# Retention with routed experts on one core: the steps in pairs, four places for rows on their way out, one for the sums

## The chip, the cores and the metric

The kernel runs on one core of one Trainium2 chip. TensorE (PE) multiplies matrices, VectorE (DVE), ScalarE (ACT) and GpSimd (POOL) work on tiles in SBUF and PSUM, and the queue of SyncE (SP) starts most transfers; ACT and POOL start some of their own. The metric is the device time of one execution in microseconds (us). Before the change the median of three runs is 399.14 us (398.21 to 399.93). A second execution, the profiled one, took 400.5 us.

## The reference

Eight heads of retention on 8 sequences of 576 tokens, then a layer of eight experts, each token going to one of them or to none:

```python
scores = scale * np.matmul(q, k.transpose(0, 1, 3, 2))
Dmat = np.where(rel >= 0, gamma[:, None, None] ** rel[None], 0.0)   # decay by distance, causal
x = np.matmul(scores * Dmat[None], v)                               # 4608 tokens x 512
do_compute = x @ w_skip > 0
e_idx = np.argmax(x @ w_gate, axis=1)                               # one expert of 8
y[mask] = gate_w * (np.maximum(xc[mask] @ w1[e], 0.0) @ w2[e])
out = x + y                                                         # y only where do_compute
```

## The kernel before, in words

The program has two parts. The first makes x, 36 tiles of 128 tokens (g = 0 to 35, nine tiles for each pair of sequences), writes it to `out` and finds each token's expert. The second runs the experts, with weights and values split into a high and a low part, three products for one. The change is in the first part alone.

**A tile.** Two transfers on SP's queue bring tile g into one of five places of `u` (`load_half`, L511): first queries and keys, then values and keys by rows. A place comes free when the tile that was five earlier is done with. PE multiplies queries by keys (`by_quarters`, L569, into `psc` and `ps_q`), and DVE and ACT put the decayed scores in place (`decay`, into `u` and `sq`). POOL scales the keys (`keys`, `kn`, L612) and the values (`rows_of`, `vs`, L634); ACT adds to `vs` the running state that PE has summed in `ps_s` (`state`, L648, copied at L663). PE then makes the tile's result in `pxt` from two groups of products, `second` (L680) and `values` (L704). `scale` (L718) is DVE's product of `pxt` with a table `gt_sb`; it puts the result into `xt`, which holds four tiles and has two places. `stage_c` (L724) turns a tile on PE (`px`), ACT copies it to `xn` (L726, two places) and asks on its own queue for the store to `out` (L727).

**A step** is one round of the loop over n and deals with two tiles; it begins with n = -1, a round without results to finish. After every second step `logits_to` multiplies the four tiles in `xt` by the gate's weights (`pl`, copied by ACT to `lt`), and in the next step `logits_from` turns the result (`pn`), reduces it on DVE (`lg`, L748) and calls `route`, whose `route_a` (L186 to L207) finds maxima and marks on DVE. `table(n)` and `growth(n)` (L544) make the tables `dq_sb` and `gt_sb` for tiles to come.

**What sets the order.** PE runs in the order in which the code is written (`tc.manual_schedule`). On the other engines a scheduler orders the operations by their needs, starting from the order of the code, and adds the waits on semaphores. Every transfer also takes one of eight lanes in turn, and waits until the lane's transfer before it has landed. PE's products are 32 bits wide, so each one in the code is two in the trace, with a load of weights each.

After the last tile PE goes to the experts: `turn_early`, `up_early`, and then up and down products in one stream (L463). That part stands as it was.

Of the kernel before, what the change touches and what calls it, by code (L numbers as in the profile page):

```python
# [12 lines left out]
F32 = mybir.dt.float32  # L13
# [10 lines left out]
NTOK, DM, NE, DF = B * S, H * D, 8, 1024  # L24
P = 128
NT = NTOK // P
HALF = S // P * 2
NQ = HALF + 1
NPR = H // 2
# [57 lines left out]
def kernel(  # L87
# [25 lines left out]
    def keep_up(n):  # L113
        for _ in range(n):
            nc.tensor.matmul(ps_m, warm[:, :P], warm, start=True, stop=True)
# [375 lines left out]
    with ExitStack() as actx:  # L491
# [35 lines left out]
        def last_product():  # L527
            return next(i for i in reversed(nc.cur_bb.bb.instructions) if i.engine == mybir.EngineType.PE)
# [18 lines left out]
        def table(n):  # L547
            times(dq_sb[:, n], mt_sb.unsqueeze(1).broadcast_to([P, NPR, D]), TQ + n, D)

        def growth(n):  # L550
            if n < NCH - 1:
                times(gt_sb[:, n], gt_sb[:, 0], TG + n, P)
            else:
                for c in range(2):
                    times(gt_sb[:, n, :, c * D : (c + 1) * D], gt_sb[:, 0, :, c * D : (c + 1) * D], TG + n + c, D)
# [23 lines left out]
        def by_quarters(g, own):  # L579
            scores(g)  # L580
            far = [score(g, 1)]
            others = itertools.chain.from_iterable(own + far if g % 2 else far + own)
            for _ in score(g, 0):
                for _ in itertools.islice(others, 1 + len(own)):
                    pass
            for _ in others:
                pass

        def decay(g):

            q = first(g)
            near, far = psc_t.pop(g)
            sc_t[g] = ap.tile([P, NPR, D], F32, tag="sq", name=f"sq_{g}", bufs=3)
            if g % 2 == 0:
                nc.vector.tensor_tensor(sc_t[g], far, dq_sb[:, g % NQ // 2], ALU.mult)
            for j in range(2):
                h = halves[1 - j]
                nc.vector.tensor_tensor(  # L598
                    u_t[g][h, j, :, :D], near[h, :, :D], mt_sb[h].unsqueeze(1).broadcast_to([D, NPR, D]), ALU.mult
                )  # L600
                if q.stop > D:
                    nc.scalar.copy(u_t[g][h, j, :, D:], near[h, :, D:])  # L602
            if g % 2:
                nc.vector.tensor_tensor(sc_t[g], far, dq_sb[:, g % NQ // 2], ALU.mult)

        def keys(g):
            i = g % NQ
            if i == HALF:
                return
            kn_t[g] = ap.tile([P, NPR, P], F32, tag="kn", name=f"kn_{g}")  # L610
            k = TK + i // 2 * 2
            nc.gpsimd.tensor_tensor(  # L612
                kn_t[g].rearrange("p a (j i) -> p a j i", j=2),
                u_t[g][:, 3].rearrange("p a (j i) -> p a j i", j=2),
                tt_sb[:, k : k + 2, :].rearrange("p j a -> p a j").unsqueeze(3).broadcast_to([P, NPR, 2, D]),
                ALU.mult,
            )
# [7 lines left out]
            for j in range(2):  # L625
                nc.gpsimd.memset(vs_t[g][halves[j], j], 0.0)

        def rows_of(g):

            if 1 < g and g % NQ < 2:  # L630
                clear(g)
            for j in range(2):
                h = halves[1 - j]
                nc.gpsimd.tensor_tensor(  # L634
                    vs_t[g][h, j],
                    u_t[g][h, 2, :, j * D : (j + 1) * D],
                    tt_sb[h, TV + g % NQ // 2, :].unsqueeze(2).broadcast_to([D, NPR, D]),
                    ALU.mult,
                )
# [50 lines left out]
        def in_turn(*products):  # L690

            products = list(products)
            while products:
                products = [p for p in products if next(p, p) is not p]
# [3 lines left out]
        def values(g):  # L698

            pxt, opens = sums(g)  # L700
            q = first(g)
            for a in range(NPR):
                for j in range(2):
                    nc.tensor.matmul(  # L704
                        pxt[halves[j], a, q],
                        vs_t[g][:, j, a, :],
                        u_t[g][:, j, a, q],
                        start=opens and a == 0,
                        stop=not opens and a == NPR - 1,
                        skip_group_check=True,  # L710
                    )
                yield

        def scale(g):
            b, o = divmod(g, NB)
            if o == 0:
                xt_t[b] = ap.tile([P, NPR, NB * P], F32, tag="xt", name=f"xt_{b}")
            nc.vector.tensor_tensor(xt_t[b][:, :, o * P : (o + 1) * P], px_t[g], gt_sb[:, g % NQ // 2], ALU.mult)  # L718

        def stage_c(g, tag="xn"):  # L720
            b, o = divmod(g, NB)
            px = pp.tile([P, DM], F32, tag=tag, name=f"px_{g}")
            for c in range(NCC):
                nc.tensor.transpose(px[:, c * P : (c + 1) * P], xt_t[b][:, c, o * P : (o + 1) * P], ident)  # L724
            xn = ap.tile([P, DM], F32, tag="xn", name=f"xn_{g}")
            nc.scalar.copy(xn.rearrange("t (p c) -> t p c", c=NCC), px.rearrange("t (c p) -> t p c", c=NCC))  # L726
            nc.scalar.dma_start(out[g * P : (g + 1) * P, :], xn)  # L727

# [15 lines left out]
        def logits_b(b, lt):  # L744
            pn = pp.tile([P, NB, P], F32, tag="xn", name=f"pn_{b}")
            for o in range(NB):
                nc.tensor.transpose(pn[:, o, :], lt[:, o * P : (o + 1) * P], ident)
            nc.vector.tensor_reduce(  # L748
                lg[:, b * NB : (b + 1) * NB, :],
                pn.rearrange("p t (c w) -> p t w c", w=WP)[:, :, :NW, :],  # L750
                axis=AX.X,
                op=ALU.add,
            )
# [100 lines left out]
        def logits_to(b, tag):  # L854
            nonlocal lt
            lt = b, logits_a(b, tag)

        def logits_from():
            nonlocal lt
            if lt is not None:  # L860
                logits_b(*lt)
                route(lt[0])
                lt = None

        def loaded(g, s, after=None):
            if 3 < g < NT:
                load_half(g, s, after)

        def have(products, g, *args):
            return [products(g)] if 0 <= g < NT else []  # L870

        def ahead(g, do):
            if 0 <= g < NT:
                do(g)
# [4 lines left out]

        for n in range(-1, NT // 2 - 1):
            e = 2 * n
            g = e + 2
            for i in range(2):
                by_quarters(e + 2 + i, have(second, e + i))
                if n < 0:
                    keep_up(NKEEP[i])
                decay(e + 2 + i)
                if n < 0:  # L890
                    keys(i)
                if i == 0:
                    loaded(e + 5, 0)
                    if n > 0:
                        scale(e)
                    if n >= 0:
                        rows_of(e + 3)
                else:
                    loaded(e + 5, 2, last_product())
            if n < 0:  # L900
                rows_of(0)
                rows_of(1)
            if 0 <= n + 2 < NCH:
                table(n + 2)
            if 0 <= n < NCH - 1:
                growth(n + 1)
            if n % 2 == 0:
                routing(1)
                logits_from()
            weights()  # L910
            in_turn(state(e + 2))
            in_turn(*([values(0)] if n == 0 else []), *have(values, e + 1))
            if n == 0:
                scale(0)
            if n >= 0:
                scale(e + 1)
            loaded(e + 6, 0)
            ahead(e + 4, keys)
            if n >= 0:
                ahead(e + 4, rows_of)  # L920
            in_turn(*have(values, e + 2 if n >= 0 else -1))
            in_turn(state(e + 3))
            loaded(e + 6, 2, last_product())
            ahead(e + 5, keys)
            if n < 0:
                rows_of(2)
            else:
                stage_c(e, "xo")
                stage_c(e + 1)
                routing(6 if g < starts[KCUT + 1] else 8)  # L930
                if n % 2:
                    logits_to(n // 2, f"sc{n % 2}")
            weights()
        g = NT
        for i in (2, 1):
# [13 lines left out]
        up_early(0)  # L949
        routing(8)  # L950
        logits_from()
        up_early(1)
        up_early(2)
        routing(8)
# [502 lines left out]
```

## Time and profile before

| what | us |
|---|---|
| median of three runs | 399.14 (398.21 to 399.93) |
| the profiled execution | 400.5 |
| its span (first to last instruction) | 398.8 |
| PE busy in the span | 363.8 |
| DVE, ACT, POOL busy | 276.4, 181.7, 151.2 |
| bytes moved | 106.15 MB |

All times of the rows below are from the span's start; 1.7 us of the execution lie outside the span. A row of a timeline gives an instruction's start, its duration, its engine and line, output and input, and in brackets how long the engine had been idle before it and what ended that. "issue" in such a place says that no semaphore was found that ended it.

### The profile page before, as it was taken

The page shows a single profiled execution, that of the slowest core. Times are in us where ns is not written, and L with a number is a line of the kernel's source. Part 1 is how long each engine was busy: PE and PEld are TensorE (multiplying, and loading weights), DVE is VectorE, ACT ScalarE, POOL GpSimd, SP SyncE. Part 2 cuts the span into 40 slices and gives each one's busy share as a digit, 9 for nine tenths or more (in the row PEclk, how much of TensorE's full clock was granted, in tenths as well). Part 3 has the DMA queues.
Part 4 walks back from the last instruction along what each step waited for, and adds up shares of the span by engine and source line. Part 5 has one row for each costly group of instructions (what it writes and reads, how often), then busy time and mean ns, then how long its engine had stood idle before and what let it go on. Part 6 is the DMA issues. An engine that isn't in the chain of part 4 may idle for free.

```text
span 398.8 us, 12381 instructions
## 1 busy us (share of the span) xinstructions
PE 363.8 (91%) x4884; PEld 335.4 (84%) x4885; DVE 276.4 (69%) x615; ACT 181.7 (46%) x369; POOL 151.2 (38%) x211
## 2 busy tenths in 40 slices
PE   7579889888989887899999999999999999999992
PEld 3477777766868776779899999999999999999992
DVE  3555677566756977696965867866867868677763
ACT  2345354454445453603743543545455545554411
POOL 5856656454754638724044200330320421101032
PEclk9999999999999999999999999999999999999997
DMA  8699999799899896607788886979789998886511
GB/s 309 260 330 315 353 324 323 245 338 341 284 339 334 308 355 217 217 29 234 226 292 256 299 236 220 319 224 353 231 257 355 307 293 284 264 279 212 159 66 59
DMA packets 49572, 106.15 MB, mean 266 GB/s; under 512 B 6102, under 2 KB 21206, under 8 KB 49511
## 3 DMA queue, kind: packets, MB, share of 16 engines
q1 hardware_dynamic: 40951, 85.81, 64.1%
q0 software_dynamic: 3232, 9.99, 7.5%
q10 hardware_dynamic: 5328, 9.52, 6.4%
q8 instruction: 40, 0.66, 0.7%
q14 instruction: 21, 0.17, 0.1%
HBM read 83.51 MB, written 22.28 MB: 265 GB/s over the span
## 4 chain that ended last, share of the span: by engine, by line
PE 57%; DMA 19%; issue 13%; DVE 5%; POOL 2%; ACT 2%; SPq 1%; ACTq 0%; POOLq 0%; DVEq 0%
PE py L463 17%; PE ph L463 16%; DMA out<-rs,sidx 8%; PE pxt L704 5%; DMA out<-xn 5%; PE ps_s L648 3%; PE psc L569 3%; DMA u<-qkv 3%; PE px L724 3%; PE pxt L680 2%; DMA xg<-out,gidx 2%; PE ps_q L569 2%; DMA xh<-hop 1%; PE pl L732 1%; PE ph_early L463 1%
## 5 line engine op out<-in xcount | busy, mean ns | idle before, releaser
L169 DVE TENSOR_TENSOR wlo_w<-w,whi_w 128x1024 fp32r<-128x1024 f32 x59 | 72.0, 1224 | 38.2 <-ACT whi_w L168 37.0
L168 ACT CAST whi_w<-w 128x1024 fp32r<-128x1024 f32 x59 | 61.7, 1049 | 32.8 <-PE py L463 31.5
L463 PE MATMUL py<-hlo,whi_w 128*128 128x336 f32 (+6 forms) x224 | 67.8, 303 | 0.0
L463 PE MATMUL ph<-xhi,wlo_w 128*128 128x336 f32 (+6 forms) x224 | 67.6, 302 | 0.0
L463 PE MATMUL ph<-xlo,whi_w 128*128 128x336 f32 (+6 forms) x224 | 67.5, 302 | 0.0
L463 PE MATMUL ph<-xhi,whi_w 128*128 128x336 f32 (+6 forms) x224 | 67.5, 301 | 0.0
L463 PE MATMUL py<-hhi,wlo_w 128*128 128x336 f32 (+6 forms) x224 | 67.5, 301 | 0.0
L463 PE MATMUL py<-hhi,whi_w 128*128 128x336 f32 (+6 forms) x224 | 67.4, 301 | 0.0
L634 POOL TENSOR_TENSOR vs<-u,tab_sb 64x256 f32<-64x256 f32 x72 | 45.0, 625 | 29.9 <-DMA u<-qkv 17.4
L1079 POOL DMA_INDIRECT out<-rs,sidx x17 | 20.8, 1223 | 83.8 <-DVE rs L1078 82.6
L612 POOL TENSOR_TENSOR kn<-u,tab_sb 128x512 f32<-128x512 f32 x32 | 34.3, 1070 | 32.4 <-DMA u<-qkv 26.2
L471 ACT ACTIVATE hhi<-ph 128x336 fp32r<-128x336 f32 (+8 forms) x61 | 25.9, 424 | 45.3 <-PE ph L463 45.0
L602 ACT COPY u<-psc 64x256 f32<-64x256 f32 x64 | 23.5, 367 | 46.4 <-DVE u L598 37.8
L569 PE MATMUL psc<-u 64*64 64x128 f32 (+1 forms) x576 | 39.1, 273 | 4.7 <-ACT lt L741 3.5
L569 PEld LDWEIGHTS psc<-u 64*64 64x64 f32 x576 | 30.0, 132 | 14.9 <-ACT xn L726 5.9
L463 PEld LDWEIGHTS ph<-xhi,whi_w 128*128 128x128 f32 x224 | 42.3, 189 | 0.1
L463 PEld LDWEIGHTS py<-hlo,whi_w 128*128 128x128 f32 x224 | 42.2, 188 | 0.2 <-DVE hlo L472 0.2
L463 PEld LDWEIGHTS ph<-xlo,whi_w 128*128 128x128 f32 x224 | 42.3, 189 | 0.1
L463 PEld LDWEIGHTS py<-hhi,whi_w 128*128 128x128 f32 x224 | 42.3, 189 | 0.0
L463 PEld LDWEIGHTS ph<-xhi,wlo_w 128*128 128x128 f32 x224 | 42.3, 189 | 0.0
L463 PEld LDWEIGHTS py<-hhi,wlo_w 128*128 128x128 f32 x224 | 42.3, 189 | 0.0
L704 PE MATMUL pxt<-u,vs 128*64 128x128 f32 (+1 forms) x576 | 34.8, 268 | 4.8 <-issue 4.1
(214 smaller groups left out, 710.8 us busy)
## 6 DMA issues: line engine op xcount, KB each, us to landing
u<-qkv SPq DMA_DIRECT2D x68, 512.0 KB
w<-w SPq DMA_DIRECT2D x64, 512.0 KB
out<-xn ACTq DMA_DIRECT2D x36, 256.0 KB
hop<-xg SPq DMA_DIRECT2D x12, 256.0 KB
xh<-hop SPq DMA_DIRECT2D x48, 64.0 KB
hopy<-yp SPq DMA_DIRECT2D x24, 128.0 KB
yr<-hopy SPq DMA_DIRECT2D x6, 512.0 KB
u<-qkv SPq DMA_DIRECT2D x4, 256.0 KB
```

The source lines that it names most:

```text
L168: nc.scalar.copy(hi, t)
L169: nc.vector.tensor_tensor(lo, t, hi.bitcast(F32), ALU.subtract)
L463: nc.tensor.matmul(ps, x, y, start=first and n == 0, stop=last and n == 3 * len(terms) - 1)
L471: nc.scalar.activation(hi, ph, AF.Relu)
L569: nc.tensor.matmul(to[halves[1 - j ^ c], a, : q.stop - q.start], u[halves[j], 1 - j, a, c * D : (c + 1) * D], u[halves[j], j, a, q], start ...
L602: nc.scalar.copy(u_t[g][h, j, :, D:], near[h, :, D:])
L612: nc.gpsimd.tensor_tensor(kn_t[g].rearrange("p a (j i) -> p a j i", j=2), u_t[g][:, 3].rearrange("p a (j i) -> p a j i", j=2), tt_sb[:, k ...
L634: nc.gpsimd.tensor_tensor(vs_t[g][h, j], u_t[g][h, 2, :, j * D : (j + 1) * D], tt_sb[h, TV + g % NQ // 2, :].unsqueeze(2).broadcast_to([D, ...
L648: nc.tensor.matmul(ps_s[halves[j], i % 2, a, :], kn_t[g][:, a, j * D : (j + 1) * D], u_t[g][:, 2, a, j * D : (j + 1) * D], start=i == 0 an ...
L704: nc.tensor.matmul(pxt[halves[j], a, q], vs_t[g][:, j, a, :], u_t[g][:, j, a, q], start=opens and a == 0, stop=not opens and a == NPR - 1, ...
L724: nc.tensor.transpose(px[:, c * P : (c + 1) * P], xt_t[b][:, c, o * P : (o + 1) * P], ident)
L1079: done = nc.gpsimd.indirect_dma_start(out=out, out_offset=bass.IndirectOffsetOnAxis(ap=idx, axis=0), in_=rs[:n], in_offset=None, bounds_ch ...
```

## The change

The loop over n now begins at 0, and what the round n = -1 did is written out ahead of it and in the round n = 0:

- The first three tiles' `vs` (tiles 0, 1 and 2, six operations of 64x256) are made by DVE, not by POOL.
- PE makes the state products of tile 0, the scores of tile 2, the state products of tile 1, and then `values(0)` ahead of the scores of tile 3. Before, both state products stood ahead of the scores, and `values(0)` and `values(1)` came alternating behind the scores of tile 3 and the state products of tile 2.
- The second half of tile 4's load waits for the state products of tile 1, as it did; the load of tile 5 is now written behind `values(0)` and its second half behind the scores of tile 3.
- `scale(e + 1)`, a step's second result, stands ahead of `table` and `growth`, and the call of `route` is a function of its own (`gates`), called behind it.
- `xn` has four places in place of two, and `xt` one in place of two.

```diff
-        def rows_of(g):
+        def rows_of(g, by=nc.gpsimd):
...
-                nc.gpsimd.tensor_tensor(
+                by.tensor_tensor(
                     vs_t[g][h, j],
...
-                xt_t[b] = ap.tile([P, NPR, NB * P], F32, tag="xt", name=f"xt_{b}")
+                xt_t[b] = ap.tile([P, NPR, NB * P], F32, tag="xt", name=f"xt_{b}", bufs=1)
...
-            xn = ap.tile([P, DM], F32, tag="xn", name=f"xn_{g}")
+            xn = ap.tile([P, DM], F32, tag="xn", name=f"xn_{g}", bufs=4)
...
         def logits_from():
+            if lt is not None:
+                logits_b(*lt)
+
+        def gates():
             nonlocal lt
             if lt is not None:
-                logits_b(*lt)
                 route(lt[0])
                 lt = None
...
-        for n in range(-1, NT // 2 - 1):
+        for g in range(2):
+            by_quarters(g, [])
+            keep_up(NKEEP[g])
+            decay(g)
+            keys(g)
+        for g in range(2):
+            rows_of(g, nc.vector)
+        table(1)
+        in_turn(state(0))
+        load_half(4, 0)
+        keys(2)
+
+        for n in range(NT // 2 - 1):
             e = 2 * n
             g = e + 2
...
+            by_quarters(e + 2, have(second, e))
+            decay(e + 2)
+            if n:
+                loaded(e + 5, 0)
+                scale(e)
+                rows_of(e + 3)
+            else:
+                in_turn(state(1))
+                load_half(4, 2, last_product())
+                keys(3)
+                in_turn(values(0))
+                load_half(5, 0)
+                scale(0)
+                rows_of(2, nc.vector)
+            by_quarters(e + 3, have(second, e + 1))
+            decay(e + 3)
+            loaded(e + 5, 2, last_product())
             if n % 2 == 0:
                 routing(1)
                 logits_from()
             weights()
-            in_turn(state(e + 2))
-            in_turn(*([values(0)] if n == 0 else []), *have(values, e + 1))
-            if n == 0:
-                scale(0)
-            if n >= 0:
-                scale(e + 1)
+            if n:
+                in_turn(state(e + 2))
+            in_turn(values(e + 1))
+            scale(e + 1)
+            if n % 2 == 0:
+                gates()
+            if not n:
+                in_turn(state(2))
+                rows_of(3)
+            if n + 2 < NCH:
+                table(n + 2)
+            if n < NCH - 1:
+                growth(n + 1)
             loaded(e + 6, 0)
             ahead(e + 4, keys)
-            if n >= 0:
-                ahead(e + 4, rows_of)
-            in_turn(*have(values, e + 2 if n >= 0 else -1))
+            ahead(e + 4, rows_of)
+            in_turn(values(e + 2))
             in_turn(state(e + 3))
             loaded(e + 6, 2, last_product())
             ahead(e + 5, keys)
-            if n < 0:
-                rows_of(2)
-            else:
-                stage_c(e, "xo")
-                stage_c(e + 1)
...
+            stage_c(e, "xo")
+            stage_c(e + 1)
```

On PE, from the scores of tile 3 to the first transposes, the program had these rows (`ps_s` are state products, `psc` and `ps_q` scores, `pxt_278` and `pxt_302` the results of tiles 0 and 1, `px` the turned tiles; the numbers are the program's names, x8 counts products):

```order
L569 MATMUL psc_299<-u_158 64x128 x2
L569 MATMUL ps_q<-u_158 64x64 x4
L648 MATMUL ps_s<-u_155,kn_245 64x64 x8
L704 MATMUL pxt_278<-u_149,vs_168 64x128 x2
L704 MATMUL pxt_302<-u_151,vs_171 64x128 x2
...
L704 MATMUL pxt_370<-u_155,vs_240 64x128 x8
L648 MATMUL ps_s<-u_158,kn_259 64x64 x8
L724 MATMUL px_393<-ident,xt_361 128x128 x4
```

Now PE has there, from the state products of tile 1 on (`pxt_262` and `pxt_310` are the results of tiles 0 and 1):

```order
L648 MATMUL ps_s<-u_151,kn_225 64x64 x8
L704 MATMUL pxt_262<-u_149,vs_168 64x128 x8
L569 MATMUL psc_307<-u_158 64x128 x2
...
L569 MATMUL ps_q<-u_158 64x64 x4
L704 MATMUL pxt_310<-u_151,vs_171 64x128 x8
L648 MATMUL ps_s<-u_155,kn_245 64x64 x8
L704 MATMUL pxt_370<-u_155,vs_240 64x128 x8
L648 MATMUL ps_s<-u_158,kn_291 64x64 x8
L724 MATMUL px_393<-ident,xt_303 128x128 x4
```

`values(0)` is in front of tile 3's scores, and from `px` on the rows are the same as before. On DVE, in the step with n = 1, the program had (`dq_sb` and `gt_sb` are tables, `xt` the results):

```order
L604 TENSOR_TENSOR sq_471<-ps_q,dq_sb 128x256
L544 TENSOR_TENSOR dq_sb<-tab_sb 128x256
L598 TENSOR_TENSOR u_295<-psc_445,tab_sb 64x4x64
L544 TENSOR_TENSOR gt_sb<-gt_sb,tab_sb 128x512
L718 TENSOR_TENSOR xt_361<-pxt_448,gt_sb 128x4x128
L595 TENSOR_TENSOR sq_577<-ps_q,dq_sb 128x256
```

And now:

```order
L604 TENSOR_TENSOR sq_471<-ps_q,dq_sb 128x256
L598 TENSOR_TENSOR u_301<-psc_445,tab_sb 64x4x64
L718 TENSOR_TENSOR xt_303<-pxt_448,gt_sb 128x4x128
L544 TENSOR_TENSOR dq_sb<-tab_sb 128x256
L544 TENSOR_TENSOR gt_sb<-gt_sb,tab_sb 128x512
L595 TENSOR_TENSOR sq_577<-ps_q,dq_sb 128x256
```

The two table operations have moved behind the result of the step; this is so in the first four steps, after which the tables are complete.

## Rows read from the trace of the kernel before

**Rows 1.** The page: busy time of engines, the instruction queue, shares of the chain
```profile
PE 363.8 (91%) x4884; PEld 335.4 (84%) x4885; DVE 276.4 (69%) x615; ACT 181.7 (46%) x369; POOL 151.2 (38%) x211
...
q8 instruction: 40, 0.66, 0.7%
...
PE 57%; DMA 19%; issue 13%; DVE 5%; POOL 2%; ACT 2%; SPq 1%; ACTq 0%; POOLq 0%; DVEq 0%
```

**Rows 2.** Windows of PE alone: us, busy (instructions), granted clock, DMA share, GB/s
```profile
0.00:163.60 163.60, 136.24 (x3269) 1.00 0.88 309
...
180.00:395.00 215.00, 211.57 (x1492) 1.00 0.77 251
```

**Rows 3.** Chain that ended last, in order of time: start, us, what
```profile
56.44 7.03 DMA out<-xn
...
73.38 8.11 DMA out<-xn
```

**Rows 4.** Timeline of ACT: copies to `xn` that came late
```profile
63.55 0.59 ACT L726 COPY xn<-px 128x512 f32<-128x512 f32 x1 [0.92 <-DMA out<-xn]
...
81.57 0.59 ACT L726 COPY xn<-px 128x512 f32<-128x512 f32 x1 [2.13 <-PE pxt L680]
```

**Rows 5.** Timeline of PE: its waits in the first 27 us
```profile
17.53 1.96 PE L704 MATMUL pxt<-u,vs 128*64 128x128 f32 x31 [1.81 <-issue]
20.16 1.07 PE L704 MATMUL pxt<-u,vs 128*64 128x128 f32 x15 [0.66 <-ACT vs L663]
...
26.10 0.27 PE L680 MATMUL pxt<-sq,u 64*64 64x64 f32 x2 [2.03 <-issue]
```

**Rows 6.** Windows, all engines: us, busy (instructions) of PE, PEld, DVE, ACT, POOL
```profile
17.53:26.09 8.56, 5.87 (x127) 5.25 (x126) 3.60 (x7) 2.99 (x8) 5.25 (x7) 1.00 0.64 217
26.09:41.36 15.27, 14.58 (x378) 12.61 (x379) 9.11 (x20) 7.80 (x19) 9.43 (x15) 1.00 0.96 336
41.37:48.39 7.02, 5.75 (x128) 4.41 (x126) 3.99 (x10) 3.03 (x7) 4.19 (x6) 1.00 0.96 340
48.40:54.19 5.79, 4.90 (x125) 4.53 (x126) 5.08 (x12) 2.39 (x7) 4.09 (x6) 1.00 0.99 348
```

**Rows 7.** Windows, all engines, as rows 6: the transfers around 18 us
```profile
14.00:16.00 2.00, 0.79 (x17) 0.66 (x18) 1.94 (x5) 0.73 (x2) 1.85 (x3) 1.00 1.02 401
16.00:18.00 2.00, 0.47 (x9) 0.46 (x10) 1.89 (x2) 0.37 (x1) 1.92 (x3) 1.00 0.19 70
18.00:20.00 2.00, 1.50 (x27) 1.25 (x22) 0.68 (x2) 0.62 (x2) 1.93 (x3) 1.00 0.00 0
...
22.00:39.00 17.00, 14.29 (x353) 12.30 (x352) 9.98 (x21) 8.88 (x22) 9.96 (x15) 1.00 0.97 335
```

**Rows 8.** Timeline of SP: the load of tile 5 and those behind it
```profile
19.44 14.43 SPq L515 DMA_DIRECT2D u<-qkv  x9
```

**Rows 9.** Timeline of DVE and POOL: operations like those that move
```profile
10.56 2.65 POOL L634 TENSOR_TENSOR vs<-u,tab_sb 64x256 f32<-64x256 f32 x4
...
16.11 1.77 DVE L544 TENSOR_TENSOR gt_sb<-gt_sb,tab_sb 128x512 f32<-128x512 f32 x1
...
42.97 0.41 DVE L544 TENSOR_TENSOR gt_sb<-gt_sb,tab_sb 128x256 f32<-128x256 f32 x1
```

**Rows 10.** Timeline of PE: its waits from 38 to 100 us
```profile
38.46 1.09 PE L724 MATMUL px<-ident,xt 128*128 128x128 f32 x8 [0.68 <-DVE xt L718]
44.69 1.10 PE L724 MATMUL px<-ident,xt 128*128 128x128 f32 x8 [0.92 <-DVE xt L718]
48.40 0.27 PE L680 MATMUL pxt<-u,sv 64*64 64x64 f32 x2 [0.36 <-issue]
...
65.29 0.33 PE L569 MATMUL psc<-u 64*64 64x128 f32 x2 [0.82 <-ACT lt L741]
...
83.20 0.33 PE L569 MATMUL psc<-u 64*64 64x128 f32 x2 [1.72 <-ACT lt L741]
...
99.44 0.33 PE L569 MATMUL psc<-u 64*64 64x128 f32 x2 [0.94 <-ACT lt L741]
```

More of the change, by code (lines that the diff above doesn't have):

```diff
@@ L878 @@
             clear(g)
-        for n in range(-1, NT // 2 - 1):
+        for g in range(2):
[10 more added lines that the diff above has]
+        for n in range(NT // 2 - 1):
             e = 2 * n
             g = e + 2
-            for i in range(2):
-                by_quarters(e + 2 + i, have(second, e + i))
-                if n < 0:
[L888 to L895, printed above, removed]
-                    if n >= 0:
-                        rows_of(e + 3)
-                else:
[L899 to L906, printed above, removed]
+            by_quarters(e + 2, have(second, e))
[15 more added lines that the diff above has]
+            loaded(e + 5, 2, last_product())
             if n % 2 == 0:
@@ L910 @@
             weights()
-            in_turn(state(e + 2))
-            in_turn(*([values(0)] if n == 0 else []), *have(values, e + 1))
-            if n == 0:
-                scale(0)
-            if n >= 0:
-                scale(e + 1)
+            if n:
[11 more added lines that the diff above has]
+                growth(n + 1)
             loaded(e + 6, 0)
             ahead(e + 4, keys)
-            if n >= 0:
-                ahead(e + 4, rows_of)
-            in_turn(*have(values, e + 2 if n >= 0 else -1))
+            ahead(e + 4, rows_of)
+            in_turn(values(e + 2))
             in_turn(state(e + 3))
@@ L924 @@
             ahead(e + 5, keys)
-            if n < 0:
-                rows_of(2)
-            else:
-                stage_c(e, "xo")
-                stage_c(e + 1)
-                routing(6 if g < starts[KCUT + 1] else 8)
-                if n % 2:
-                    logits_to(n // 2, f"sc{n % 2}")
+            stage_c(e, "xo")
+            stage_c(e + 1)
+            routing(6 if g < starts[KCUT + 1] else 8)
+            if n % 2:
+                logits_to(n // 2, f"sc{n % 2}")
             weights()
@@ L951 @@
         logits_from()
+        gates()
         up_early(1)
```

## The prediction
> **What bounds the kernel now.** I read the page first, then windows of PE, then the chain in order of time, then PE's waits in the first part. The page has PE busy 363.8 of 398.8 us, and the chain goes through PE for 57% [rows 1]. The windows split that. From 180 to 395 us PE is busy 211.57 of 215 us: the experts are one stream of products, and I found no wait in it that the change could touch. In the first 163.6 us PE is busy 136.24 us [rows 2]. So the experts end as much earlier as the first part does, and the question is which of the first part's waits last.
>
> The chain shows two transfers of `xn` to `out` there, 7.03 and 8.11 us long [rows 3]: with two places, a copy to `xn` waits until the store of two tiles earlier has landed. The copies came 0.92 and 2.13 us late for it [rows 4]; the second row names PE, whose products are no input of the copy, so the store is what it waited for. ACT copies `lt` behind them, and PE waits for that: 0.82, 1.72 and 0.94 us [rows 10].
>
> But there is a second bound, and the sum hangs on it. Between the pauses at 17.53, 26.10, 48.40 and 54.19 us that nothing in the program explains (1.81, 2.03 and 0.36 us at the first three) stand 127 + 126 instructions of PE and PEld, then 378 + 379 and 128 + 126 in the stretches on either side of 41.37 us, then 125 + 126 [rows 5, 6, 10]. With a few instructions of the sequencer, which the windows do not count, these are 256, three times 256, 256 and 256. The page has a queue for instructions with 40 transfers of 0.66 MB together, 16 KB each [rows 1], so 64 bytes an instruction. I read it so: PE gets its program in blocks of 256 instructions, through the same transfer engines as the tiles, and pauses where a block is late. A wait that is taken away just ahead of such a pause gives nothing: PE comes sooner to a block that comes no sooner.
>
> The transfers are close to full, too: a share of 0.97 at 335 GB/s from 22 to 39 us. Ahead of that stands a hole: 0.19 from 16 to 18 us and 0.00 from 18 to 20 us, 3.6 us of all engines [rows 7], because the load of tile 5 starts at 19.44 us only [rows 8]. It needs tile 0's place in `u`, and `values(0)` stands behind the pause of 17.53 us [rows 5].
>
> **The start.** PE now makes `values(0)` ahead of the scores of tile 3. As many instructions as before stand ahead of the turned tiles, so the block boundary of 17.53 us is at the same instruction; what lies in front of it has changed, and `values(0)` is now there. I take the block to come when it did, since the loads in the queue ahead of it are the same. Then nothing that PE gains before 17.53 us counts, but `values(0)` is done before it, and the load of tile 5 is asked for some 4 to 5 us sooner than at 19.44 us, into the hole. Behind the boundary stand as many instructions up to the scores of tile 4 as before, without the wait of 0.66 us for ACT's `vs` [rows 5], because the state products of tiles 1 and 2 now come further ahead of their users: 0.66 us. The next boundary is the pause of 2.03 us at 26.10 us. Tile 5's two loads, which I take to have been in front of that block, are then out of the way, and the block can come while PE still works: 2.03 us more. Together 2.69 us. Bounds: 0, if the block comes when it did before, and 3.6 us, the hole, if all that the transfers gain comes through; the pieces that the rows show are nearest to the middle of it, and I keep 2.69.
>
> For this the values of tiles 0 to 2 move to DVE, six operations. The trace has none of them on DVE. The nearest is a table operation on 128x256 with both inputs in SBUF, 0.41 us; the other side is the 128x512 one that took 1.77 us beside POOL's work [rows 9]. So six cost 2.5 to 10.6 us of DVE; I take 0.41, as the shapes agree. DVE has the time: what it delays is the scores' part for tile 1, hence PE's scores of tile 2, by under 1 us, and that lies ahead of the block at 17.53 us, which waits for more than it. POOL loses as much (2.65 us for four [rows 9]) and gets to tile 2's and 3's keys sooner. If that cover were gone, DVE's delay would count in full, up to 1 us. On DVE the values also stand in order behind a load's landing (tile 2's), with `scale(0)` queued behind them; nobody needs that before the turned tiles.
>
> **The stores.** Four places for `xn` let a copy wait for the store of four tiles, two steps earlier; a step takes some 8 us, the stores 7 to 8 [rows 3], so the copies' wait goes. The three waits for `lt` are 0.82 + 1.72 + 0.94 = 3.48 us [rows 10]. Of the third, less than half may be the store's. At the boundaries behind them PE shows no pause, so their blocks came in time, but how long before they were needed no row tells. Bounds 0 and 3.48; I take the middle, 1.74 us. What is late next is that block, or the copy itself behind ACT's other work.
>
> **`scale` ahead of the tables.** Two waits of PE for `xt`, 0.68 and 0.92 us, lie in the first steps, where two table operations stood ahead of `scale` on DVE. The pause at 48.40 us is the next thing behind the second, and its block is awaited [rows 10]. So I count nothing; bounds 0 and 1.60 us. The call of `gates` behind `scale` moves little: in the order of DVE's instructions the gates' operations interleave with `scale` nearly as before.
>
> **One place for `xt`.** The first result of four now overwrites what the logits' products read. Those stand on PE ahead of the next scores, and `scale` comes behind the scores on DVE, so the wait is over when it is asked: nothing. Without that cover it would be one wait in every second step.
>
> **Sum**: 2.69 + 1.74 = 4.43 us. The profiled execution took 400.5 us (span 398.8), so 396.1 by its own time. It lies 1.4 us above the median of 399.14, of which the same gain leaves 394.7.
>
> The Trainium skill, page "Runtime: NRT & Kernel Launch", section "Instruction fetch mechanics", also has 16 KiB blocks of 256 instructions that the sequencer asks for itself, but calls the cost of crossing a boundary "mostly hidden". Here it is not: 1.81 and 2.03 us at two of the first boundaries [rows 5]. By that rule the waits would count in full, which is rival A.
>
> **Rivals.**
> - A: the blocks are no bound once the queue is less full, and every wait counts: 2.69 + 1.60 + 3.48 = 7.77 us, 391.4. For it: at three boundaries behind the `lt` waits no pause shows. Against: the stretches of 256 end in pauses before and after.
> - B: the blocks, or the loads at a share of 0.97, take back nearly all. PE comes sooner to things that come no sooner; what is left is the 0.66 us and little more, say 1 us: 398.1. For it: the pause at 48.40 us follows at once on the waits of 38.46 and 44.69 us. Against: the hole of 3.6 us in the transfers is real, and a fuller queue early is time gained if the transfers are the bound.
> - C, slower: loads that start sooner and stores that no longer wait put more transfers in front of each block. A block that comes later stops PE at the boundary, one to one. With about 25 blocks of which I take 17 to be awaited, a delay of 0.26 us each eats the 4.43 us, and 0.5 us each gives 8.5 - 4.43 = 4.1 us more: 403.2. For it: the pauses already spread from 0.36 to 2.03 us. Against: the total of bytes is the same, and the queue's length is set by five places of `u` as before.
> - D: the scheduler undoes it, the rest as before: 399.1. The order of PE is as written, so this is open only for DVE and ACT.
>
> **Chances.** Forecast 0.45 (own range 393 to 396.8), A 0.22, B 0.22, C 0.08, D 0.03. What can be told from no change is about 0.5%, 2 us: faster is under 397.1, slower over 401.1. Faster: the forecast, A and a little of B, 0.70; same: B but for that, D, a little of C, 0.22; slower 0.08. The range for 8 in 10 goes from 389.8, where A also has the hole's rest and a little more, to 399.9, which takes in B and D.
>
> **What would show it.** Right: tile 5's load starts near 14 us and no window of 2 us before 22 us has a share near 0; PE's scores of tile 4 start about 1 us sooner, and the pause of 2.03 us is gone or under 0.5; no copy to `xn` waits for a store; the waits for `lt` shrink, and some come back as pauses marked "issue" at the same instructions; the experts' stream starts 4 to 5 us sooner and is as long. Wrong: the first block comes at another time than 17.53 us, or the pauses after it add up to more than they did, or the experts' part changes its length.

## The result, and the profile after

| | median us | lowest to highest | runs |
|---|---|---|---|
| before | 399.53 | 396.67 to 406.51 | 12 |
| changed | 395.94 | 392.62 to 399.72 | 12 |

The ratio is 0.9885, with a 95% interval from 0.9844 to 0.9926. On 399.53 us that is 4.6 us less (3.0 to 6.2); forecast were 4.43. In a second comparison (label again, below) it was 0.9873 (0.9827 to 0.9919). The two profiled runs of the changed kernel took 399.12 and 397.94 us, above their medians, and that of before took 400.5, so single traces show less of the gain than the medians do; the section on the hardware says what lies between. The ratios leave out runs more than 1.5% above the fastest of their kernel, so the medians of the table lie only 3.6 us apart, and of one kernel below, the start alone, two of six runs are left (the other four took 399.35 to 399.59 us).

The page of the changed kernel: busy time, and the shares of the chain.

```profile
PE 363.9 (92%) x4884; PEld 336.1 (85%) x4885; DVE 280.7 (71%) x621; ACT 181.3 (46%) x369; POOL 146.3 (37%) x205
...
PE 60%; DMA 14%; issue 13%; DVE 8%; POOL 1%; ACT 1%; SPq 1%; POOLq 0%; DVEq 0%; ACTq 0%
```

PE does as much as before [rows 1]. DVE has six operations more and POOL six fewer. The share of transfers in the chain falls from 19% to 14%.

PE alone in the first part of the changed kernel: us, busy (instructions), clock, share of the transfers, GB/s.

```profile
0.00:160.70 160.70, 136.39 (x3269) 0.99 0.90 315
```

The same 3269 instructions as in [rows 2], as busy, in 2.9 us less. The experts' first product stands at 160.84 us, before at 163.69. From there to the end of the span are 236.5 us in this trace, 234.9 in the second one and 235.1 before, so this part differs by more than 1 us from trace to trace of one kernel, and this trace loses there half of what it gained.

PE's pauses in the first trace of the changed kernel, and that first product.

```profile
17.32 0.98 PE L704 MATMUL pxt<-u,vs 128*64 128x128 f32 x13 [0.97 <-issue]
23.78 0.27 PE L680 MATMUL pxt<-sq,u 64*64 64x64 f32 x2 [1.03 <-issue]
34.78 1.08 PE L704 MATMUL pxt<-u,vs 128*64 128x128 f32 x15 [0.81 <-issue]
41.17 0.27 PE L569 MATMUL psc<-u 64*64 64x128 f32 x1 [1.88 <-issue]
...
160.84 0.39 PE L463 MATMUL ph_early<-x,whi_w 128*128 128x256 f32 x1 [1.42 <-DVE x L174]
```

The first block comes at 17.32 us, before at 17.53, and the second at 23.78, before at 26.10 [rows 5]: 2.3 us gained by then. The pauses there are 0.97 and 1.03 us, no longer 1.81 and 2.03.

Tile 5's load on SP's queue, and the windows of all engines that had the hole.

```profile
15.04 0.33 SPq L515 DMA_DIRECT2D u<-qkv  x1
```

```profile
14.00:16.00 2.00, 2.00 (x67) 1.76 (x62) 1.62 (x3) 1.39 (x4) 1.16 (x2) 1.00 1.06 350
16.00:18.00 2.00, 1.03 (x14) 0.79 (x16) 1.94 (x4) 0.23 (x1) 1.85 (x3) 1.00 0.81 264
18.00:20.00 2.00, 1.94 (x45) 1.73 (x42) 1.98 (x4) 1.21 (x4) 1.38 (x2) 1.00 0.97 344
```

The load starts 4.4 us sooner than in [rows 8], and the shares of 0.19 and 0.00 [rows 7] are 0.81 and 0.97.

From 40 to 48 us the same trace shows what took the gain back for a while (PE alone, columns as above).

```profile
40.00:42.00 2.00, 0.83 (x15) 0.96 0.85 255
42.00:44.00 2.00, 2.00 (x31) 0.50 0.97 308
44.00:46.00 2.00, 2.00 (x28) 0.69 0.86 320
46.00:48.00 2.00, 2.00 (x54) 1.00 0.88 273
```

Behind the pause of 1.88 us the granted clock is at 0.50, its lower level of 1.2 GHz, for 3.4 us in all. The turned tiles that follow start at 44.92 us, before at 44.69 [rows 10].

### The profile page after: what moved, and what is told of

It is laid out like the page before. It is cut to its first block, busy times and chain, and to the rows that moved or that the text cites. A ratio compares the mean times of both kernels' runs of the same rounds, so it can differ in the third digit from the quotient of the medians.

```text
span 397.4 us, 12378 instructions
## 1 busy us (share of the span) xinstructions
PE 363.9 (92%) x4884; PEld 336.1 (85%) x4885; DVE 280.7 (71%) x621; ACT 181.3 (46%) x369; POOL 146.3 (37%) x205
## 4 chain that ended last, share of the span: by engine, by line
PE 60%; DMA 14%; issue 13%; DVE 8%; POOL 1%; ACT 1%; SPq 1%; POOLq 0%; DVEq 0%; ACTq 0%
PE py L463 16%; PE ph L463 15%; DMA out<-rs,sidx 8%; PE pxt L704 6%; PE px L724 4%; PE psc L569 4%; PE ps_s L648 4%; PE pxt L680 3%; PE pl L732 2%; PE ps_q L569 2%; DMA xg<-out,gidx 2%; DMA u<-qkv 2%; DVE u L598 1%; DMA w<-w 1%; DMA hop<-xg 1%
## 5 line engine op out<-in xcount | busy, mean ns | idle before, releaser
L634 POOL TENSOR_TENSOR vs<-u,tab_sb 64x256 f32<-64x256 f32 x66 | 41.2, 625 | 25.4 <-DMA u<-qkv 10.3
L569 PE MATMUL psc<-u 64*64 64x128 f32 (+1 forms) x576 | 38.2, 272 | 5.8 <-issue 3.2
L704 PE MATMUL pxt<-u,vs 128*64 128x128 f32 (+1 forms) x576 | 36.0, 274 | 5.8 <-issue 5.8
```

The source lines that it names most:

```text
L569: nc.tensor.matmul(to[halves[1 - j ^ c], a, : q.stop - q.start], u[halves[j], 1 - j, a, c * D : (c + 1) * D], u[halves[j], j, a, q], start ...
L634: by.tensor_tensor(vs_t[g][h, j], u_t[g][h, 2, :, j * D : (j + 1) * D], tt_sb[h, TV + g % NQ // 2, :].unsqueeze(2).broadcast_to([D, NPR, D ...
L704: nc.tensor.matmul(pxt[halves[j], a, q], vs_t[g][:, j, a, :], u_t[g][:, j, a, q], start=opens and a == 0, stop=not opens and a == NPR - 1, ...
```

## The experiments

All ratios are to the kernel before, timed on the same chip. There were three chips: one for again and the parts alone, one for after_xn2, after_pool, filler and shift, one for the rest. "Changed" edits start from the changed kernel, "before" edits from the kernel before.

**A second look: again.** No edit.

> The changed kernel as it is, once more, for a second trace. Its ratio to before was 0.9885 (0.9844 to 0.9926), and its first trace shows one stretch, 42 to 46 us, in which the granted clock fell to 0.50 behind a pause of PE of 1.88 us; the gain of 2.3 us that the start had brought was gone by 45 us. If that fall is an accident of one run, the second trace has none before 160 us, the turned tiles of the second step (36.4 us there) and of the third (44.9) come 2 to 3 us sooner than before's 38.46 and 44.69, and the experts' stream starts at 158 to 160 us (before 163.69). If it belongs to the new order, the same pause and the same fall come again near 41 us. Ratio 0.985 to 0.992 either way.

Measured: 0.9873 (0.9827 to 0.9919). PE's pauses in this second trace, and the first product of the experts:

```profile
34.24 1.08 PE L704 MATMUL pxt<-u,vs 128*64 128x128 f32 x15 [0.83 <-issue]
41.50 1.09 PE L724 MATMUL px<-ident,xt 128*128 128x128 f32 x8 [0.61 <-DVE xt L718]
45.92 0.27 PE L680 MATMUL pxt<-u,sv 64*64 64x64 f32 x1 [1.01 <-issue]
...
113.48 2.20 PE L704 MATMUL pxt<-u,vs 128*64 128x128 f32 x31 [2.54 <-issue]
...
161.33 0.39 PE L463 MATMUL ph_early<-x,whi_w 128*128 128x256 f32 x1 [1.41 <-DVE x L174]
```

No pause and no fall near 41 us, and the turned tiles are at 41.50 us, 3.2 us sooner than before. So that fall belongs to one run and not to the new order. But this run has others, at 12 us and behind the pause at 113.48, and two parts of the expectation were wrong: no fall before 160 us, and the experts' stream at 158 to 160 us (161.33).

**The parts alone.** Three kernels: the new start with everything else as before; in the kernel before, the places alone; in the kernel before, the order of the tables alone.

```diff
# start_only, against the changed kernel
-xt_t[b] = ap.tile(..., bufs=1)
+xt_t[b] = ap.tile(...)
-xn = ap.tile(..., bufs=4)
+xn = ap.tile(...)
+            if n + 2 < NCH: table(n + 2)
+            if n < NCH - 1: growth(n + 1)
             if n % 2 == 0:
                 routing(1)
                 logits_from()
+                gates()
...
             scale(e + 1)
-            if n % 2 == 0: gates()
-            if n + 2 < NCH: table(n + 2)
-            if n < NCH - 1: growth(n + 1)
# xn4_xt1, against the kernel before
+xt: bufs=1, xn: bufs=4
# scale_only, against the kernel before
-            if 0 <= n + 2 < NCH: table(n + 2)
-            if 0 <= n < NCH - 1: growth(n + 1)
...
                 scale(e + 1)
+            if 0 <= n + 2 < NCH: table(n + 2)
+            if 0 <= n < NCH - 1: growth(n + 1)
```

> Of the change only the new start: values of tiles 0 to 2 on VectorE, values(0) ahead of the scores of tile 3, tile 5's load behind it. Places of xn and xt, the tables and the gates are as before. The prediction's split: 2.69 us less, ratio 0.9933, with the scores of tile 4 near 21.4 us and the second block near 23.8 us as in the changed kernel, and the waits for lt still there (0.8, 1.7, 0.9 us). If each wait counts in full: 2.7 to 3.6 us, 0.991 to 0.993. If the blocks and the full transfer queue take the early gain back: under 1 us, 0.9975 to 1.0, with longer pauses marked issue between 26 and 60 us.

> Of the change only the places: four for xn and one for xt; the rest as before. The prediction's split: 1.74 us less, ratio 0.9956, the copies to xn never late for a store, the waits of PE for lt gone or halved and half of that back as pauses marked issue behind them. If each wait counts in full: 3.48 us, 0.9913. If the blocks take all back: 0, 1.000. If one place for xt costs something: PE or DVE wait at the first result of every second step, and the ratio is over 1.000.

> Of the change only the order on VectorE: the result of a step's second tile ahead of the table operations of the first four steps; the places and the start as before. The prediction's split: 0, ratio 1.000, since the waits for xt at 38.46 and 44.69 us (0.68 and 0.92 us) go and come back as a longer pause at the block behind them (48.40 us, 0.36 us before). If each wait counts in full: 1.60 us, 0.996.

Measured: start 0.9835 (0.9768 to 0.9902) from two runs, and 0.992 if the mean of all six, 397.65, is set against the mean of before, 400.82; places 0.9954 (0.9920 to 0.9989); order 0.9974 (0.9937 to 1.0011). The start alone gains, 3.2 us by the second number, but six runs are few: its median, 399.38, is only 1.1 us below that of before. The places gain 1.8 us (0.4 to 3.2), which is the prediction's number. The order can't be told from nothing.

**The places, taken back.** In the changed kernel, xn with two places; then xn and xt with two; and in the kernel before, one place for xt alone.

```diff
# after_xn2, against the changed kernel
-xn: bufs=4
# start_scale, against the changed kernel
-xn: bufs=4, xt: bufs=1
# xt1_only, against the kernel before
+xt: bufs=1
```

> The changed kernel with two places for xn again, all else as changed. If the stores cost what the prediction's sum has (1.74 us) and the parts add up: ratio to before 0.991 (start and scale alone), the copies to xn late for stores again by up to 2 us near 65, 80 and 98 us, and PE waiting for lt there. If the changed kernel's blocks hide the stores anyway: no change against the changed kernel, 0.987.

> The changed kernel with two places for xn and two for xt: the new start and the results ahead of the tables, without the change of places. If one place for xt is free, this is the same as the changed kernel with xn alone put back (0.998, 0.994 to 1.002). If the parts add up as each alone had it (start 0.9835 to 0.992, scale 0.997): 0.989 to 0.991. In either case the copies to xn are late for stores near 65, 80 and 98 us.

> The kernel before with one place for xt in place of two, all else as before. Four places for xn with one for xt gave 0.9954, and the changed kernel loses 2 to 3 us when xn alone goes back to two places, so one place for xt may cost what the four places bring. If it costs nothing, as predicted: ratio 1.000, and no operation of VectorE that writes a first result of four waits for the logits' products. If it eats part of the stores' gain: 1.003 to 1.005, with waits of VectorE for the logits' products in every second step.

Measured: 0.9980 (0.9939 to 1.0021), 0.9952 (0.9906 to 0.9998) and 1.0040 (1.0002 to 1.0078). Who waits for whom (us in total, times, longest), first in the kernel with two places for xn:

```profile
ACT xn L726 <- DMA out<-xn: 6.1, 6, 2.3
...
PE psc L569 <- ACT lt L741: 3.1, 2, 2.3
```

then with two for xn and two for xt:

```profile
ACT xn L726 <- DMA out<-xn: 5.8, 4, 3.1
...
PE psc L569 <- ACT lt L741: 4.1, 3, 2.7
```

and in the second trace of the changed kernel, with four:

```profile
PE px L724 <- DVE xt L718: 3.8, 4, 1.6
...
PE psc L569 <- ACT lt L741: 0.9, 2, 0.5
```

With four places no copy waits for a store in either trace of the changed kernel, and PE's wait for `lt` is 0.9 us in this one and none in the other; with two it is 3 to 4 us, as in [rows 10]. So the places for xn bring, inside the changed kernel, 0.9980 - 0.9873 = 0.0107, 4.3 us (1.8 to 6.8 from both intervals), more than the 1.74 that the sum had. These two ratios come from different chips. Two kernels below that keep four places and ran on the same chip as this one (0.9893 and 0.9879) give 3.5 and 4.0; their medians, 394.89 and 394.74 us against 398.98, give 4.1 and 4.2. One place for xt loses 1.6 us (0.1 to 3.1) alone. The step from 0.9952 to 0.9980 doesn't confirm it: the intervals overlap, and the medians go the other way (401.48 of 401.26 us, and 398.98 of 399.88). If the loss is taken from xn4_xt1, 3.4 us are left for xn, near the full 3.48. Where xt's loss is, no row shows: one place leaves the order on every engine as it was, and VectorE's first results of four wait for no product of the logits. It stays open, and with an interval that just clears 1 it may be smaller or nothing.

**VectorE or GpSimd for the first values, and PE's wait at 12 us.** The values of tiles 0 to 2 by GpSimd again; six wide warm-up products in PE's idle time; both, with three.

```diff
# after_pool, against the changed kernel
-rows_of(g, nc.vector)
+rows_of(g)
-rows_of(2, nc.vector)
+rows_of(2)
# filler, against the changed kernel
         in_turn(state(0))
+        keep_up(6)
         load_half(4, 0)
# pool_filler: both, with keep_up(3)
```

> The changed kernel with the values of tiles 0 to 2 on GpSimd again, all else as changed. If the move to VectorE is free, as predicted, this one is later: values(0) waits for vs of tile 0 behind the keys of tiles 0 to 2 on GpSimd, tile 5's load starts near 16 us rather than 14, and the time is 0.5 to 2 us over the changed kernel's, ratio 0.989 to 0.992. If the move costs more than it brings (PE waits 1.8 us at 11.9 us in the changed kernel for the copy behind VectorE's scores of tile 1, before it waited 1.2), this one is faster, ratio 0.983 to 0.986.

> The changed kernel with six of the wide warm-up products (0.2 us each) between the state products of tile 0 and the scores of tile 2, where PE was idle for 1.80 us in both traces of the changed kernel. In the second trace the granted clock then fell to 0.50 from 12 to 15 us. If a pause is what lets the clock fall and the fall costs about half of 3.2 us at the start, none is seen before 16 us here and PE reaches the first turned tiles up to 1.5 us sooner in runs that had it; in the mean 0.5 to 1 us less, ratio 0.984 to 0.986. If the early time is hidden by the block at 17 us anyway: no change, 0.987. If the products themselves are in the way: up to 0.5 us more.

> The changed kernel with the values of tiles 0 to 2 on GpSimd and three wide warm-up products (0.2 us each) behind the state products of tile 0, where that version had 0.73 us of idle PE left. If what the two variants gained (0.9893 and 0.9879, both traces ending at 392.2 us) is that the granted clock stays up at the start, this is no better than either: 0.987 to 0.989. If VectorE's relief and the clock are two gains, 0.983 to 0.985, faster than the changed kernel by 1 us or more.

Measured: 0.9893 (0.9830 to 0.9955), 0.9879 (0.9836 to 0.9923) and 0.9881 (0.9816 to 0.9945). None can be told from the changed kernel. VectorE at the start of the second trace of the changed kernel:

```profile
8.00 1.62 DVE L634 TENSOR_TENSOR vs<-u,tab_sb 64x256 f32<-64x256 f32 x2 [0.16 <-DMA u<-qkv]
9.65 0.43 DVE L598 TENSOR_TENSOR u<-psc,tab_sb 64x256 f32<-64x256 f32 x1
...
10.57 0.42 DVE L634 TENSOR_TENSOR vs<-u,tab_sb 64x256 f32<-64x256 f32 x1
11.02 0.42 DVE L598 TENSOR_TENSOR u<-psc,tab_sb 64x256 f32<-64x256 f32 x1
```

The values stand among the decayed scores of tile 1, ACT's copy comes behind those, and PE waits 1.80 us for it. With GpSimd PE waits less there, and as much more at `values(0)`:

```profile
10.57 0.33 PE L569 MATMUL psc<-u 64*64 64x128 f32 x2 [0.76 <-DMA u<-qkv]
16.67 0.55 PE L704 MATMUL pxt<-u,vs 128*64 128x128 f32 x6 [1.99 <-POOL vs L634]
```

The row names POOL, but 1.99 us end at the first block's boundary, 16.67 us, like the 0.97 us at 17.32 in the changed kernel. The filler does what it was put there for. Windows of PE in the second trace of the changed kernel, and with the filler:

```profile
12.00:14.00 2.00, 2.00 (x52) 0.50 1.02 402
14.00:16.00 2.00, 2.00 (x38) 0.73 0.77 282
```

```profile
12.00:14.00 2.00, 2.00 (x76) 1.00 1.04 403
14.00:16.00 2.00, 1.42 (x52) 1.00 1.01 343
```

But both kernels reach the first turned tiles at the same time, 20.12 and 20.00 us, and the first trace of the changed kernel, which has no fall there, at 20.42. PE is merely busy for longer ahead of a block that comes when it comes.

**Where the blocks end: shift.** 128 instructions more ahead of everything, while PE waits for the first load.

```diff
-    keep_up(NWARM)
+    for _ in range(NWARM + 64):
+        nc.tensor.matmul(ps_m[:, :64], warm[:, :P], warm[:, :64], start=True, stop=True)
```

> The changed kernel with 73 narrow products (64 columns) in the place of the 9 wide ones with which TensorE warms up while the first load is on its way: 128 instructions more ahead of everything else, in time that PE waits anyway. If the pauses marked issue stand where a block of 256 instructions ends, all of them move 128 instructions ahead in the program: none at the places of the second trace of the changed kernel (29.3 us at scores, 34.2 at values, 45.9 at second, 79.0 at second, 130.3 at values), others half a block earlier, and the first one near 13 to 15 us in place of 17. The time may move either way by about 1 us, ratio 0.984 to 0.990. If the pauses belong to the operations or the loads at those places, they stay at the same operations.

Measured: 0.9983 (0.9944 to 1.0022), slower than the changed kernel by 1% in the ratios and by 0.6% in the medians beside filler on the same chip (397.17 against 394.74 us); its trace has the clock at 0.50 from 12 to 19 us and again from 36 us. Windows from the start to four of its longer pauses (us, busy and instructions of PE, PEld and the others, as in [rows 6]):

```profile
0.00:34.46 34.46, 27.21 (x602) 23.04 (x602) 20.98 (x39) 13.55 (x33) 19.38 (x47) 0.90 0.88 315
0.00:52.62 52.62, 43.38 (x981) 37.06 (x982) 32.13 (x66) 20.50 (x50) 28.64 (x62) 0.90 0.86 304
0.00:87.46 87.46, 73.95 (x1741) 63.42 (x1742) 57.31 (x135) 37.21 (x92) 47.55 (x90) 0.94 0.88 314
0.00:125.00 125.00, 108.17 (x2628) 93.09 (x2628) 81.84 (x202) 56.66 (x140) 69.80 (x122) 0.96 0.89 317
```

and to three of the second trace of the changed kernel:

```profile
0.00:34.23 34.23, 28.28 (x599) 21.81 (x601) 20.17 (x45) 15.00 (x37) 21.59 (x50) 0.95 0.90 335
0.00:45.90 45.90, 38.34 (x853) 30.29 (x854) 27.24 (x58) 19.84 (x48) 28.26 (x60) 0.96 0.91 330
0.00:113.47 113.47, 98.54 (x2372) 82.05 (x2374) 75.64 (x187) 52.78 (x130) 67.27 (x118) 0.98 0.93 328
```

PE and PEld together: 1204, 1963, 3483 and 5256 with the shift, 1200, 1707 and 4746 without. The steps between them are 759, 1520 and 1773, and 507 and 3039: 3, 6, 7, 2 and 12 times 253, which with the sequencer's few is 256. The count at a pause is the same grid in both, though the program is 128 instructions on. The pause at a count of 1200 was at `values` and is at `second` now (one line further down in this kernel's file, so L681):

```profile
34.47 0.27 PE L681 MATMUL pxt<-sq,u 64*64 64x64 f32 x1 [1.83 <-issue]
```

So the pauses belong to the ends of blocks and not to operations. The transfers of the instruction queue say the same: in the first trace of the changed kernel four of them land at 15.99, 22.44, 33.33 and 39.71 us, and the pauses end at 17.32, 23.78, 34.78 and 41.17 us, 1.3 to 1.5 us behind each. The first pause was not seen near 13 to 15 us. There PE was at half its clock, and a later PE may wait for no block; that is argued, not shown.

**What the blocks wait behind: less_bytes.** The keys by rows are not loaded; their place in the running state takes the values.

```diff
-            n = 1 if s and g % NQ == HALF else 2
+            n = 1 if s else 2
...
-                u_t[g][:, 3].rearrange("p a (j i) -> p a j i", j=2),
+                u_t[g][:, 2].rearrange("p a (j i) -> p a j i", j=2),
```

> The changed kernel without the loads of the keys by rows: the second half of each tile brings the values only (256 KB less for each of 32 tiles), and GpSimd scales the values in the keys' place, so the running state is another; instructions on all engines are as many as in the changed kernel. If blocks of instructions come late because loads stand ahead of them in the queue: the pauses marked issue in the first part, 7.4 and 11.7 us together in the two traces of the changed kernel, fall below 3 us, and the experts' stream starts 5 to 8 us sooner (161 us before). If a block takes as long whatever the queue holds (about 1 us, asked for too late): the pauses stay at 7 us or more and the stream starts at most 2 us sooner.

Only the first part can be compared, since the tokens go to other experts (439.98 us in all). All rows over 0.3 us that are marked issue from 12 us on, and the first product of the experts:

```profile
40.16 0.45 PE L569 MATMUL ps_q<-u 64*64 64x64 f32 x7 [2.02 <-issue]
68.02 0.69 PE L648 MATMUL ps_s<-u,kn 128*64 128x64 f32 x16 [0.34 <-issue]
99.91 0.69 PE L648 MATMUL ps_s<-u,kn 128*64 128x64 f32 x16 [1.06 <-issue]
129.18 0.69 PE L648 MATMUL ps_s<-u,kn 128*64 128x64 f32 x16 [1.17 <-issue]
...
155.64 0.39 PE L463 MATMUL ph_early<-x,whi_w 128*128 128x256 f32 x1 [1.41 <-DVE x L174]
```

The first trace of the changed kernel has ten such rows. Of the four here only the first stands where a block ends. The two at 68.02 and 99.91 us stand at the same products in the changed kernel (0.35 us at 69.43 in one trace, 1.06 at 99.29 in the other) wherever the blocks end, and the one at 129.18 stands 4101 instructions of PE and PEld behind the first, 16.2 times 253. With a pause of 0.24 us at 145.10 us, 19 times 253 behind the first, the pauses at ends of blocks are 2.3 us together. In the two traces of the changed kernel they are 11.8 and 7.4 us, in the other traces here with all the loads 5.1 to 13.3. So with less in the queue fewer blocks are late enough to be seen, and that speaks for blocks that are late because of what stands ahead of them; it rests on one trace. The start of the experts says nothing on it: it is 5.2 and 5.7 us sooner than in the two traces of the changed kernel, but it is as early in those of after_pool and filler (155.61 and 155.68 us), which have all the loads.

## Why the prediction was right, step by step

**The sum was right** (4.43 us forecast, 4.6 and 5.1 measured), and so was the place, the first part. The sign that the experts' stream starts 4 to 5 us sooner is not met in either trace of the changed kernel (2.9 and 2.4 us); in those of after_pool, filler and pool_filler, which can't be told from it in time, it starts 6.5 to 8.1 us sooner. And two of the sum's terms, the stores and the one place for `xt`, were off and offset each other, so that it came this close was in part luck.

- *The start, 2.69 us.* The boundary at 17.53 us stayed (17.32), `values(0)` is done ahead of it, the load of tile 5 fills the hole, the scores of tile 4 are 1.3 us sooner (21.44 us; before 22.76), and the second block is 2.3 us sooner. The pause there was to be under 0.5 us; it is 1.03 us in one trace and not to be seen in the other. That the gain comes from the load in the hole and not from the new order of products alone is argued from these rows; no run has the one without the other. With the order of the tables this part measures 1.9 us (0.1 to 3.8) in start_scale, and 3.2 us alone in start_only.
- *The values on VectorE, at nothing.* Right in the time and for the reason given. Six took 0.41 to 1.18 us each, 3.3 together in the second trace. The scores of tile 2 are later by 0.2 and 0.6 us, ahead of a block for which PE waits in any case, and on GpSimd the time is the same.
- *The stores, 1.74 us.* This term was probably too small. The mechanism was right, but half of the waits for `lt` was taken off for blocks behind them, and the runs with two and four places put it at 3.4 to 4.3 us (1.8 to 6.8 by the widest interval), which is near the full 3.48 of rival A. Where no pause stands at a boundary, its block has slack, and that should have counted for the wait ahead of it.
- *`scale` ahead of the tables, 0.* No change that can be told: 0.9974 (0.9937 to 1.0011). The waits for `xt` did not go; they moved from the two places of [rows 10] to others, and are 3.6 and 3.8 us together in the two traces (2.2 in that of before by the same view). In the second trace PE waits 1.19 us for `xt` at 52.02 us, and VectorE had this ahead of the `scale` that writes it:

```profile
49.44 1.67 DVE L192 SCALAR_TENSOR_TENSOR oh<-ls,desc 128x64 f32<-128x64 f32 x1
51.14 0.22 DVE L196 TENSOR_REDUCE m<-oh 128x8 f32<-128x64 f32 x1
51.28 0.68 DVE L718 TENSOR_TENSOR xt<-pxt,gt_sb 128x512 f32<-128x512 f32 x1
```

  The gates are called behind `scale` and still run ahead of this one, as the prediction had read from the order of VectorE's instructions.
- *One place for `xt`, 0.* Measured as a loss of 1.6 us (0.1 to 3.1) alone. No row has it, so it isn't explained, and its interval just clears nothing.

**Rival A** (every wait counts) holds, as far as the intervals tell, for the stores and not for the blocks, which go on ending PE's work on the grid of 256. **Rival B** fell: the queue doesn't take the early gain back. **Rival C** fell for the time as a whole, but its mechanism exists: the one trace of less_bytes speaks for blocks that are late because of what is queued ahead of them. The Trainium skill, page "Runtime: NRT & Kernel Launch", section "Instruction fetch mechanics", calls the crossing of a block "mostly hidden": with less_bytes that is nearly what the trace shows (pauses of 2.02 and 0.24 us at 25 ends of blocks), and with the full queue of the changed kernel it is not (0.97, 1.03, 0.81 and 1.88 us in the first 42 us). By these two kernels the full queue decides.

No version beats the changed kernel: after_pool, filler and pool_filler have ratios within 0.002 of it.

## What to carry to other kernels

Before a wait is counted as a gain, look whether the engine pauses a little later with nothing named, at a multiple of a fixed count of instructions: in this kernel 1.8 us less of waiting just ahead of such a pause gave nothing that could be measured (filler), while the waits ahead of boundaries without a pause counted about in full. Where the transfers are nearly full, look for a hole in them first, and for bytes to leave out before instructions to move. Judge a part of 1% by many runs, since the first part of one trace can hold four falls of the clock (start_scale) and that of another none (before, filler).

## What the runs showed of the hardware

- **The clock falls in some runs and not in others, at the same place of one kernel.** In the first trace of the changed kernel the fall of 42 us costs this: from the turned tiles at 36.36 us to the next at 44.92 are 8.56 us, in the second trace, without a fall, 5.68 (35.82 to 41.50). Of the 2.88 us between them 1.27 are the longer pause (1.88 against 0.61), and the other 1.6 are about half of the 3.4 us at half the clock. In the first parts of all the traces here a pause of 1.2 to 3.1 us comes ahead of each fall, but not behind each pause a fall: 1.80 us at 12 us is followed by one in the second trace of the changed kernel, 1.81 us in the first is not, and the trace of before has none in the first part, with pauses of 2.03 and 1.81 us [rows 5].
- **A run's mean clock and its time go together in some kernels.** The trace of before has a mean granted clock of 0.995; the 23 runs of before beside again, on another chip, have 0.975 to 0.994. The third of them with the lowest clock (0.979 in the mean) took 402.3 us in the mean, the third with the highest (0.990) 399.6. But in the 12 runs of the changed kernel nothing of it is to be seen: the fastest, 392.62 us, has 0.987, and two with 0.991 took 399.12 and 399.72 us. And before's profiled run took 400.5 us, over the median, with a clock above those of all 23. So a run's mean clock belongs beside its time, but it does not stand for it.
